# Decaying attention in front of two expert layers: leaving out the scores above the diagonal blocks, and letting the planner choose among ten plans

## The chip, the cores and the metric

One core of one Trainium2 chip runs the kernel, in one launch. The metric is the device time of that launch in microseconds (us). The engines are TensorE (PE: matmuls; its weight loads have a row of their own, PEld), VectorE (DVE), ScalarE (ACT), GpSimd (POOL) and SyncE (SP), which here only issues DMAs.

## What is computed

Three stages, one behind the other. The first is attention with a decay: for 2 batches and 8 heads of 64 columns, in blocks of 64 positions out of 768,

```python
intra = (qb @ kb.T * Dmask) @ vb          # Dmask = lam ** (i - j) for i >= j, else 0
inter = (qb * lam_pow) @ kv_state
out[block] = intra + inter
kv_state = lam ** 64 * kv_state + (kb * rev_pow).T @ vb
```

Then `x = out` as 1536 tokens of 512 columns goes through `(sigmoid(x @ w_gate) * (x @ w_val)) @ w_out` with 1536 hidden columns, and through `elu(x @ w_in) @ w_out2` with 2048.

## The kernel before

**Attention** goes in six chunks of 128 positions (`CH`; the loop of line 595), so two of the reference's blocks are one chunk, and the mask of a chunk is 128 by 128. Chunk `c` has two loads of 1 MB (`load`, line 535): `tin`, k and q with head columns on partitions, and `nat`, k and v with positions on partitions. For a chunk the program does:

- `scores` (line 582): for each batch, 16 fp32 matmuls give k by q of all heads, `st`, in two row tiles (heads in partitions 0 to 63 and 64 to 127) that write two PSUM banks, `A1` and `B1`. DVE multiplies each bank by the decay mask `da` into `pr`. The second batch uses the same two banks.
- `kd`, k with its decay, 8 ACT instructions; `ql`, q with its decay, 2 on POOL.
- `u`, 32 matmuls of `kd` by v into bank `C1`, and on DVE the state `sn` for the next chunk.
- `x`, 32 matmuls of v by `pr`, whole 128 by 128 blocks, into banks `xu_0` and `xu_1`, and from the second chunk on 32 more of the state by `ql` on top, these in four 64x64 tiles of the array (`x<-ql,sn` in the rows; `xs` below).
- `split_chunk` (line 444) reads `x` on ACT, DVE and POOL and makes the operands of the first expert layer, each split into a high and a low part (`x11h`, `x11l` and so on).

**The expert layers** multiply in fp32r, three matmuls for one product of split operands. `product` (line 479) is a seven-multiplication scheme for 2x2 blocks: groups M2, M5, M1, M4, M3, M7, M6 of six matmuls each. M2, M4, M7 add up in bank A, M5, M3, M6 in bank B, and M1 has bank C; between groups ACT and DVE read the banks. In the profile bank `A0` is called `warm`, since that tile came first. After chunks 1, 3 and 5 the products G and V (gate and value) of 256 columns of the first weight group run. `unit` (line 687) is the product with `w_out`: six matmuls of up to 512 columns into `xu`, two banks, which attention's `x` uses before. A weight block of 1 MB comes in as 64-bit words through one buffer `w64`, and `fetch` and `prep_sums` turn it into operands on ACT, DVE and POOL.

**Order.** Every operation is recorded by a helper, so all rows say line 177. `issue` (line 314) then makes the order of each engine's instructions: `run` (line 256) is a list scheduler with costs for each operation, used forward and backward five times in turn; the plan with the earliest end is kept. `together` makes one operation of a block of matmuls; `hazards` (line 200) finds who must wait for whom, for PSUM by bank and partition half. 24 matmuls on zeros (`warm<-idle`) are recorded ahead of all.

The buffers tie the stages together: `tin` and `nat` of chunk 3 go where those of chunk 0 were, chunk 4's where chunk 1's were, chunk 5's where chunk 3's were. `pr`, `ql` and `xa` lie in the buffers that the operands of `w_out` (`woh`, `wol`) take later.

Of the kernel before, what the change touches and what calls it, by code (L numbers as in the profile page):

```python
# [110 lines left out]
class Op:  # L111
    __slots__ = ("eng", "call", "reads", "writes", "gap", "took", "port", "table", "preds", "shape")
# [12 lines left out]
class Work:  # L125
# [10 lines left out]
    def cost(self, op, fn, args, kw):  # L136
# [4 lines left out]
        if op.eng == "tensor":  # L141
            dt = kw["rhs"].dtype
            op.shape = dt if dt != F32 else (kw["lhsT"].halves, kw["lhsT"].ix.size) if len(kw["rhs"].halves) < 2 else kw["lhsT"].ix.size
# [5 lines left out]
        if op.eng == "sync":  # L149
            return 440, n * P * 4 / 423  # L150
# [11 lines left out]
    def record(self, eng, fn, args, kw):  # L162
# [13 lines left out]
        def call():  # L176
            return getattr(getattr(self.nc, eng), fn)(*(real(a) for a in args), **{k: real(a) for k, a in kw.items()})  # L177
# [7 lines left out]
    def together(self, ways=2):  # L185
# [11 lines left out]
        op.call = lambda: [c() for c in calls][-1]  # L197
        self.ops.append(op)

    def hazards(self):  # L200
        write, read, banks, tables = {}, {}, {}, {1: [], 2: []}
        holder, users, freed = {}, {}, {}
        for k, op in enumerate(list(self.ops)):
# [46 lines left out]
            if op.table:  # L250
                before.update(tables[3 - op.table])
                tables[op.table].append(k)
            before -= {-1, k}
            op.preds = sorted(before)

    def run(self, preds, key, backward=False):
# [7 lines left out]
        at, start, end = [0.0] * n, [0.0] * n, [0.0] * n  # L264
        free = dict.fromkeys(ENGINES, 0.0)
        port = behind = queue = 0.0
        shape = table = None
        for k in range(n):
            if not left[k]:
                heapq.heappush(soon[ops[k].eng], (0.0, k))  # L270
        for _ in range(sum(op.eng is not None for op in ops)):
# [5 lines left out]
            k = heapq.heappop(ripe[e])[1]  # L277
            op = ops[k]
            if e == "sync":
                late = 300 if queue < t + 2000 else 1100  # L280
# [33 lines left out]
    def issue(self, tc, rounds=5):  # L314
# [7 lines left out]
        key, best = list(range(n)), None  # L322
        for _ in range(rounds):
            start, end = self.run(preds, key)
            if best is None or max(end) < best[0]:
                best = (max(end), start)
            _, back = self.run(turned, [-end[n - 1 - k] for k in range(n)], True)
            key = [-back[n - 1 - k] for k in range(n)]
        order = sorted(range(n), key=lambda k: (best[1][k], k))
        behind = mybir.DependencyInfo(mybir.DependencyClass.Sync, mybir.DependencyReason.DATA)  # L330
        port = None
        with tc.manual_schedule():
            for k in order:
                op = self.ops[k]
                made = op.call()
                if op.eng and op.port:
                    if op.eng == "vector":
                        port = made
                    elif port:
                        tc.add_manual_dep(made.ins, port.ins.name, behind, reason="shared port")  # L340
                        port = None
# [3 lines left out]
def tile_decay_attention_two_mlps(  # L345
# [133 lines left out]
    def product(kind, w, ops, sig, r, which, gsplit=None):  # L479
        s, t0, n = r  # L480
        bank, wt = {}, None
        for m in ORDER:
            x = BANK[m]
            if x not in bank:
                bank[x] = ps.tile([P, 512], F32, BANKS[which][x])[:, :n]
# [3 lines left out]
            first = m in ("M2", "M5", "M1")  # L489
# [4 lines left out]
            if m == "M2":  # L494
                wt = sb.tile([P, NS[which]], F32, f"wt{which}", bufs=2)[:, :n]
                nc.scalar.copy(wt, p)
            elif m == "M5":
# [27 lines left out]
    da = low[:, 0:1024].rearrange("p (q g n) -> p q g n", q=2, g=NP)  # L525
    lp = low[:, 1024:1536].rearrange("p (g n) -> p g n", g=NP)
    rev = da[:, :, :, CH - 1:CH]
    l_ch = lp[:, :, CH - 1:CH]

    lam_s = sb.tile([P, H + NP], F32, "lam")  # L530
    nc.sync.dma_start(out=lam_s, in_=lam2)
# [3 lines left out]
    def load(c):  # L535
        if c == 2:
            tin[c] = sb.tile([P, 2, 2, NP, CH], F32, "xPh1", name="tin2")
            nat_of[c] = sb.tile([P, 2, 2, H, D], F32, "sig1", name="nat2")
        else:
            tin[c] = sb.tile([P, 2, 2, NP, CH], F32, ("gh1", "gl1")[int(c in (1, 4))], name="tin")  # L540
        to = tin[c].rearrange("p b q g s -> p b (q g s)")
        for b in (slice(0, 1), slice(1, 2)) if not c else (slice(0, 2),):
            nc.sync.dma_start(out=to[:, b], in_=att[c, 0][:, b])
        nc.sync.dma_start(out=nat_of[c].rearrange("p b q h e -> p b (q h e)"), in_=att[c, 1])
# [11 lines left out]
    one = low[:, 1536:1536 + CH]  # L556
    nc.gpsimd.memset(one, 1.0)
    nc.gpsimd.affine_select(out=one, in_=one, pattern=[[1, CH]], compare_op=ALU.is_equal, fill=0.0,
                            base=1 - CH, channel_multiplier=1)
    for h in range(H):  # L560
        nc.vector.tensor_tensor_scan(out=da[:, h // NP, h % NP], data0=lam_s[:, h:h + 1].to_broadcast([P, CH]),
                                     data1=one, initial=0.0, op0=ALU.mult, op1=ALU.add)
    nc.vector.tensor_copy(lp[:, :, 0], lam_s[:, H:H + NP])
# [7 lines left out]
    for _ in range(24):  # L571
        nc.tensor.matmul(warm, lhsT=idle[:, :P], rhs=idle, start=True, stop=True)

    xops = [new_xops(0), new_xops(1)]
    kds, prs, sns, xas = {}, {}, {}, {}
# [3 lines left out]
    def half(q, p):  # L579
        return (q + p // 2) % 2  # L580

    def scores(c):
        prs[c] = []
        for b in range(2):
# [6 lines left out]
            for q in range(2):  # L591
                nc.vector.tensor_tensor(out=pr[:, q], in0=sts[q], in1=da[:, q], op=ALU.mult)
            prs[c].append(pr)

    for c in range(NCH):
        more = c + 1 < NCH
        s, t0 = (0, c * CH) if c < 2 else (1, (c - 2) * CH)
        scores(c)
        if more:
            kd = sb.tile([P, 2, H, D], F32, ("gh0", "gl0")[c % 2], name="kd")  # L600
            for h in range(H):
                nc.scalar.mul(kd[:, :, h], nat_of[c][:, :, 0, h], rev[:, half(h % 2, h // 2), h // 2])
        if c:
            ql = sb.tile([P, 2, NP, CH], F32, "wol_0", name="ql")
            for b in range(2):
                nc.gpsimd.tensor_tensor(out=ql[:, b], in0=tin[c][:, b, 1], in1=lp, op=ALU.mult)
        if more:
            u = ps.tile([P, 2, NP, D], F32, "C1", name="u")
            with nc.together():
                for b in range(2):  # L610
                    for p in range(NP):
                        for q in range(2):
                            nc.tensor.matmul(u[(lo, hi)[half(q, p)], b, p], lhsT=kd[:, b, 2 * p + q],
                                             rhs=nat_of[c][:, b, 1, 2 * p + q], start=True, stop=True)
            sn = sns[c + 1] = sb.tile([P, 2, NP, D], F32, f"wt1_{c % 2}", name="sn")
            if c == 0:
                nc.vector.tensor_copy(sn, u)
            else:
                for p in range(NP):
                    nc.vector.scalar_tensor_tensor(out=sn[:, :, p], in0=sns[c][:, :, p], scalar=l_ch[:, p],  # L620
                                                   in1=u[:, :, p], op0=ALU.mult, op1=ALU.add)
# [235 lines left out]
```

## Time and profile before

| | |
|---|---|
| time, median of 3 runs | 593.93 us (593.72 to 594.12) |
| the profiled execution's own time | 593.81 us |
| its span, first to last instruction | 592.1 us |
| what lies around the span | 1.7 us |
| PE, DVE, POOL, ACT busy | 98%, 66%, 53%, 51% of the span |
| DMA | 51.98 MB, 51.39 MB of it through one queue |

The ends of matmuls are modelled, so a busy PE is not PE at its peak: how long a block of matmuls takes is read from where it starts to where the next one starts. In the chain of work, a piece is such a stretch. A timeline row gives start and duration in us, then engine, operation, tiles (out<-in), shapes and count, and in brackets the idle time before it with what ended it.

### The profile page before, as it was taken

How to read it: one execution, taken by the hardware profiler on the slowest of the kernel's cores; microseconds unless marked ns; L12 is line 12 of the kernel's file. 1: busy time of each engine (PE TensorE's matmuls, PEld its weight loads, DVE VectorE, ACT ScalarE, POOL GpSimd, SP SyncE). 2: the span in 40 equal slices, each digit the busy share in tenths (PEclk: the TensorE clock that was granted, in tenths of full speed). 3: DMA queues.
4: the chain of work that ended last, by engine and by line, in shares of the span. 5: the costliest groups of instructions: out<-in, count | busy, mean ns of one | idle time of the engine just before them, and what ended most of it. 6: DMA issues, size and time to landing. Idle time of an engine off the chain costs nothing.

```text
span 592.1 us, 9322 instructions
## 1 busy us (share of the span) xinstructions
PE 582.0 (98%) x3632; PEld 496.2 (84%) x3632; DVE 389.6 (66%) x690; ACT 300.5 (51%) x571; POOL 313.3 (53%) x264
## 2 busy tenths in 40 slices
PE   9999989999999999999999999999999999999997
PEld 5788878888888888888898888887888888888886
DVE  5978653566467457457548985667666777777484
ACT  3884356543343244243247988755636454646160
POOL 2778398478476376367237884563805446361100
PEclk9999999999999999999999999999999999999999
DMA  8945022222212211122202202312221111110004
GB/s 320 417 190 214 2 71 73 81 103 102 72 71 72 71 72 72 71 73 71 72 2 72 72 0 83 132 72 71 72 72 43 53 53 68 72 71 1 0 37 178
DMA packets 8828, 51.98 MB, mean 88 GB/s; under 512 B 1104, under 2 KB 1360, under 8 KB 3024
## 3 DMA queue, kind: packets, MB, share of 16 engines
q1 hardware_dynamic: 8784, 51.39, 23.5%
q8 instruction: 28, 0.46, 0.3%
q14 instruction: 16, 0.13, 0.1%
HBM read 48.24 MB, written 3.15 MB: 87 GB/s over the span
## 4 chain that ended last, share of the span: by engine, by line
PE 85%; ACT 4%; DMA 4%; DVE 4%; POOL 3%; issue 1%; ACTq 0%; POOLq 0%; SPq 0%; DVEq 0%
PE xu L177 37%; PE B L177 19%; PE A L177 11%; PE warm L177 10%; PE C L177 6%; DMA w<-in_w_val 2%; DMA w<-in_w_in 2%; ACT w L177 1%; PE x L177 1%; DVE sums L177 1%; PE st L177 1%; ACT sig L177 1%; POOL l L177 1%; DVE w L177 1%; ACT kd L177 1%
## 5 line engine op out<-in xcount | busy, mean ns | idle before, releaser
L177 PE MATMUL xu<-gh,woh 128*128 128x512 f32 (+1 forms) x322 | 126.0, 395 | 1.6 <-DVE xt L177 1.4
L177 PE MATMUL xu<-gl,woh 128*128 128x512 f32 (+1 forms) x322 | 126.0, 391 | 0.0
L177 PE MATMUL xu<-gh,wol 128*128 128x512 f32 (+1 forms) x322 | 125.3, 389 | 0.0
L177 DVE TENSOR_TENSOR acc<-xu,acc 128x512 f32<-128x512 f32 x120 | 81.2, 687 | 39.9 <-PE xu L177 39.0
L177 POOL TENSOR_TENSOR gl<-sig,gh 128x1024 fp32r<-128x1024 f32 (+1 forms) x38 | 73.2, 1938 | 53.3 <-ACT gh L177 33.3
L177 POOL TENSOR_TENSOR t<-w 128x512 f32<-128x512 f32 (+1 forms) x80 | 69.0, 889 | 42.7 <-DVE w L177 40.0
L177 POOL TENSOR_TENSOR l<-t,h 128x768 fp32r<-128x768 f32 (+1 forms) x38 | 61.0, 1615 | 41.3 <-DVE w L177 19.7
L177 PEld LDWEIGHTS xu<-gh,woh 128*128 128x128 f32 x322 | 60.5, 188 | 15.6 <-DVE xt L177 1.4
L177 PEld LDWEIGHTS xu<-gh,wol 128*128 128x128 f32 x322 | 60.5, 188 | 12.1
L177 PEld LDWEIGHTS xu<-gl,woh 128*128 128x128 f32 x322 | 60.6, 188 | 11.8 <-POOL gl L177 1.2
L177 POOL TENSOR_TENSOR wol<-w,woh 128x512 fp32r<-128x512 f32 x26 | 33.1, 1293 | 59.8 <-ACT woh L177 59.2
L177 ACT CAST gh<-sig 128x512 fp32r<-128x512 f32 (+1 forms) x58 | 45.2, 784 | 33.9 <-DVE sig L177 32.5
L177 ACT ACTIVATE w<-w 128x1024 f32<-128x1024 f32 x34 | 38.6, 1135 | 34.8 <-POOL wol L177 18.2
L177 DVE SCALAR_TENSOR_TENSOR w<-w,w 128x1024 uint32<-128x1024 uint32 x34 | 46.5, 1367 | 0.3
L177 DVE TENSOR_TENSOR wt<-B,wt 128x256 f32<-128x256 f32 (+1 forms) x45 | 22.9, 509 | 33.7 <-PE B L177 31.7
L177 DVE TENSOR_SCALAR w<-w 128x1024 uint32<-128x1024 uint32 x34 | 31.2, 916 | 21.0 <-ACT w L177 20.6
L177 ACT ACTIVATE sig<-B 128x256 f32<-128x256 f32 (+1 forms) x62 | 28.3, 456 | 29.5 <-PE B L177 24.2
L177 ACT ACTIVATE sig<-warm 128x256 f32<-128x256 f32 x36 | 13.9, 385 | 49.1 <-DVE warm L177 24.5
L177 DVE TENSOR_TENSOR wt<-C,wt 128x256 f32<-128x256 f32 (+1 forms) x45 | 23.0, 511 | 18.9 <-PE C L177 18.3
L177 ACT ACTIVATE sig<-sig 128x256 f32<-128x256 f32 (+1 forms) x68 | 34.5, 507 | 1.6
L177 ACT CAST h<-t 128x512 fp32r<-128x512 f32 (+1 forms) x40 | 29.1, 728 | 8.7 <-PE B L177 4.5
L177 POOL TENSOR_TENSOR l<-w,h 128x256 fp32r<-128x256 f32 x36 | 26.7, 752 | 9.5 <-ACT h L177 4.1
(143 smaller groups left out, 1477.1 us busy)
## 6 DMA issues: line engine op xcount, KB each, us to landing
w<-in_w_out SPq DMA_DIRECT2D x14, 1024.0 KB, 4.8
w<-in_w_in SPq DMA_DIRECT2D x8, 1024.0 KB, 4.7
nat<-in_att SPq DMA_DIRECT2D x6, 1024.0 KB, 11.7
w<-in_w_gate SPq DMA_DIRECT2D x6, 1024.0 KB, 5.3
w<-in_w_val SPq DMA_DIRECT2D x6, 1024.0 KB, 4.9
tin<-in_att SPq DMA_DIRECT2D x5, 1024.0 KB, 12.1
out_t<-o SPq DMA_DIRECT2D x11, 256.0 KB, 2.0
tin<-in_att SPq DMA_DIRECT2D x2, 512.0 KB, 5.0
```

The costliest lines, as they stand in the source:

```text
L177: return getattr(getattr(self.nc, eng), fn)(*(real(a) for a in args), **{k: real(a) for k, a in kw.items()})
```

## The change

- **Scores in 64-position blocks.** Of a chunk's 128 by 128 scores of a head, the three 64 by 64 blocks that the mask doesn't zero are made, with 64x64 tiles of the array, four at a time. The work is grouped by four heads (`g`) of both batches in place of one batch: group 0 uses banks `A1`, `B1`, group 1 `C0`, `C1`. A group is 16 matmuls, eight of 128 columns and eight of 64. `pr` has 3/4 of the elements.
- **`x`** is made in two parts: the first 64 positions from one 64 by 64 block (16 matmuls of 64 rows, four tiles), the others from all 128 rows (16 matmuls with 64 columns out).
- **`u` of chunk c-1** is made in `scores(c)`, in two halves, in columns 384 to 511 of the score banks. For chunk 1 ACT copies it (four instructions) where DVE had one.
- A small ACT instruction per chunk stands between the first part of `x` and the matmuls of the state (`fence`).
- **`product`, in the attention stage,** goes M5, M2, M1, ... on two banks: M1 has the second half of bank B (`two=True`).
- **`unit`** of the first weight group puts its first eight results into banks `C0`, `C1`.
- **Loads** of chunks 0 to 2 come in halves of 512 KB; `lam` is loaded through ACT's queue. Loads of chunks 3, 4, 5 are recorded behind `scores` of chunks 1, 2, 4 (before: behind chunks 0, 1, 3).
- The mask is set up by eight scans (four of 128, four of 64 columns), six ACT copies.
- 18 matmuls on zeros in place of 24.
- **The planner** tries ten settings of two new parameters (`stick`: stay with a matmul shape; `ahead`: don't start an operation long before it is due), seven rounds each, takes the DMA queue as busy until 3.5 us, and counts each change between matmul forms as before (150 ns).

```diff
-    def issue(self, tc, rounds=5):
+    def issue(self, tc, rounds=7):
...
+        best = None
+        for stick in (0, 1500, 4000, 10000, 20000):
+            for ahead in (8e3, 20e3):
+                key, gate, least = list(range(n)), None, 1e9
+                for _ in range(rounds):
+                    start, end = self.run(preds, key, gate=gate, stick=stick)
...
-    def product(kind, w, ops, sig, r, which, gsplit=None):
+    def product(kind, w, ops, sig, r, which, gsplit=None, two=False):
...
-        for m in ORDER:
+        for m in ("M5", "M2") + ORDER[2:] if two else ORDER:
...
+                if two and x == 2:
+                    bank[x] = bank[1, "rest"]
...
+            for cols in (slice(0, 1024), slice(1024, 2048)) if c < 3 else (slice(0, 2048),):
+                nc.sync.dma_start(out=to[:, cols], in_=src[:, cols])
...
-            pr = sb.tile([P, 2, NP, CH], F32, f"woh_{b}", name="pr")
-            sts = [ps.tile([P, NP, CH], F32, bank, name="st") for bank in ("A1", "B1")]
-            with nc.together():
-                for p in range(NP):
-                    for st, r in zip(sts, (lo, hi)):
-                        nc.tensor.matmul(st[:, p], lhsT=tin[c][r, b, 0, p], rhs=tin[c][r, b, 1, p], start=True, stop=True)
...
+        for g in range(2):
+            pr = sb.tile([P, 2, 2, 3, 64], F32, f"woh_{g}", name="pr")
+            banks = [ps.tile([P, 512], F32, bank, name="st") for bank in (("A1", "B1"), ("C0", "C1"))[g]]
+            sts = [t[:, 0:384].rearrange("p (b t n) -> p b t n", b=2, t=3) for t in banks]
+            with nc.together(4):
+                for b in range(2):
+                    k, q = (tin[c][:, g, b, i].rearrange("p i (t n) -> p i t n", n=64) for i in range(2))
+                    for full in (True, False):
+                        for st, r in zip(sts, (lo, hi)):
+                            for p in range(2):
+                                at = (hi, lo) if full == (p == 0) else (lo, hi)
+                                ts = (slice(0, 3, 1 + p) if p else slice(0, 2)) if full else slice(1 + p, 2 + p)
+                                nc.tensor.matmul(st[at[0], b, ts], lhsT=k[r, p, int(full)],
+                                                 rhs=q[r, p] if full else q[r, p, 1:2], start=True, stop=True)
+            u = [t[:, 384:512].rearrange("p (b e) -> p b e", b=2) for t in banks]
+            if c:
+                with nc.together():
...
+                                nc.tensor.matmul(u[i][(lo, hi)[half(q, i)], b], lhsT=kds[c - 1][:, b, h],
+                                                 rhs=nat_of[c - 1][:, 1, b, h], start=True, stop=True)
...
+                            nc.tensor.matmul(xs[i][r, b, g, 0:64], lhsT=nat_of[c][at, 1, b, 2 * p + q],
+                                             rhs=prs[c][g][at, half(q, p), b, 0], start=b == 0 and g == 0 or not c,
...
+                            nc.tensor.matmul(xs[i][r, b, g, 64:128], lhsT=nat_of[c][:, 1, b, 2 * p + q],
+                                             rhs=prs[c][g][:, half(q, p), b, 1 + i], start=not c,
...
+            nc.scalar.mul(low[:, 1667 + c:1668 + c], low[:, 1664:1665], 1.0)
+            work.ops[-1].fence = quads
...
-            product("G", wG, xops, sig, r, 0)
-            product("V", wV, xops, sig, r, 0)
+            product("G", wG, xops, sig, r, 0, two=True)
+            product("V", wV, xops, sig, r, 0, two=True)
...
-        units(wo, g, adder(acc, i == 1))
+        units(wo, g, adder(acc, i == 1), early=2 if i == 1 else 0)
```

## Rows read from the trace of the kernel before

**Rows 1.** The page's busy time: engine, us, share of the span, instructions.
```profile
PE 582.0 (98%) x3632; PEld 496.2 (84%) x3632; DVE 389.6 (66%) x690; ACT 300.5 (51%) x571; POOL 313.3 (53%) x264
```

**Rows 2.** Stretches of the span: length, busy us of PE, PEld, DVE, ACT, POOL, clock, DMA.
```profile
7.10:25.70 18.60, 17.68 (x250) 13.54 (x249) 13.85 (x26) 12.95 (x38) 9.34 (x8) 1.00 1.01 423
25.70:39.10 13.40, 12.69 (x174) 10.90 (x170) 10.49 (x24) 11.06 (x28) 9.56 (x8) 1.00 0.70 283
39.10:72.80 33.70, 33.20 (x430) 29.71 (x430) 25.89 (x65) 14.37 (x34) 21.57 (x16) 1.00 0.31 114
...
98.00:310.00 212.00, 212.00 (x1163) 184.27 (x1162) 123.06 (x195) 85.31 (x143) 120.97 (x106) 1.00 0.21 75
310.00:350.00 40.00, 38.75 (x235) 33.92 (x235) 36.20 (x86) 33.98 (x79) 32.41 (x31) 1.00 0.16 53
...
440.00:588.70 148.70, 148.62 (x734) 124.98 (x732) 102.64 (x159) 71.51 (x121) 50.50 (x38) 1.00 0.15 54
```

**Rows 3.** The chain that ended last, in order of time: start, us, what.
```profile
21.58 11.48 DMA w<-in_w_val
...
39.64 1.08 PE u L177 x32
...
43.39 1.09 PE st L177 x16
46.47 2.93 PE x L177 x64
...
60.12 1.02 PE x L177 x16
...
66.11 1.03 PE x L177 x32
```

**Rows 4.** Timeline, 3 to 26 us: ahead of the first product G.
```profile
3.20 0.71 SPq L177 DMA_DIRECT2D w<-in_w_gate  x1
...
18.03 3.77 ACT L177 ACTIVATE kd<-nat,low 128x128 f32<-128x128 f32 x12
...
18.48 2.79 PE L177 MATMUL u<-nat,kd 128*64 128x64 f32 x31
...
23.19 0.60 ACT L177 CAST h<-t 128x512 fp32r<-128x512 f32 x1
...
25.75 0.38 PE L177 MATMUL warm<-x11h,h 128*128 128x256 f32 x1
```

**Rows 5.** Timeline, 34 to 40 us: ahead of the first product V.
```profile
34.32 1.28 ACT L177 ACT_TABLE_LOAD   x1
...
38.66 0.42 ACT L177 ACTIVATE sig<-warm 128x256 f32<-128x256 f32 x1
...
39.13 0.39 PE L177 MATMUL warm<-x11h,h 128*128 128x256 f32 x1 [0.30 <-ACT sig L177]
```

**Rows 6.** Timeline, 50 to 53 us: from the first product V to the second G.
```profile
50.15 0.28 PE L177 MATMUL B<-xPh,l 128*128 128x256 f32 x1
...
50.47 0.43 DVE L177 TENSOR_TENSOR B<-B,wt 128x256 f32<-128x256 f32 x1 [0.28 <-PE B L177]
...
52.13 0.42 DVE L177 TENSOR_TENSOR sig<-B,sig 128x256 f32<-128x256 f32 x1
```

**Rows 7.** Timeline of PE, 72 to 77 us: the end of attention.
```profile
72.83 1.10 PE L177 MATMUL x<-ql,sn 64*64 64x128 f32 x32
74.72 0.39 PE L177 MATMUL warm<-x11h,h 128*128 128x256 f32 x1 [0.79 <-ACT x11h L177]
...
76.61 0.47 PE L177 MATMUL xu<-gh,woh 128*128 128x512 f32 x1 [0.45 <-DVE xt L177]
```

**Rows 8.** The tile `pr`: ns min/median/max, first and last start.
```profile
L177 DVE TENSOR_TENSOR pr<-st,low x24: 676/682/693, 8.3 to 70.0; 128x512 f32<-128x512 f32 x24
```

**Rows 9.** The tile `x`, the same columns.
```profile
L177 DVE TENSOR_TENSOR x22l<-x,x22h x6: 416/417/419, 17.1 to 76.4; 128x256 fp32r<-128x256 f32 x6
```

**Rows 10.** The page's DMA issues: count, KB of each, median us to landing.
```profile
w<-in_w_out SPq DMA_DIRECT2D x14, 1024.0 KB, 4.8
```

More of the change, by code (lines that the diff above doesn't have):

```diff
@@ L111, with __init__ @@
 class Op:
-    __slots__ = ("eng", "call", "reads", "writes", "gap", "took", "port", "table", "preds", "shape")
+    __slots__ = ("eng", "call", "reads", "writes", "gap", "took", "port", "table", "preds", "shape", "fence")
+    def __init__(self):
+        self.fence = None
 class Engine:
@@ L184, in together @@
     @contextmanager
-    def together(self, ways=2):
+    def together(self, ways=2, fence=None):
         self.block = []
@@ L252, in hazards, with run @@
                 tables[op.table].append(k)
+            if op.fence:
+                before.add(self.ops.index(op.fence))
             before -= {-1, k}
             op.preds = sorted(before)
-    def run(self, preds, key, backward=False):
+    def run(self, preds, key, backward=False, gate=None, stick=0):
         ops = self.ops[::-1] if backward else self.ops
@@ L263, in run @@
         ripe, soon = {e: [] for e in ENGINES}, {e: [] for e in ENGINES}
-        at, start, end = [0.0] * n, [0.0] * n, [0.0] * n
+        at, start, end = [max(0.0, g) for g in gate] if gate else [0.0] * n, [0.0] * n, [0.0] * n
         free = dict.fromkeys(ENGINES, 0.0)
-        port = behind = queue = 0.0
+        port = behind = 0.0
+        queue = 3500.0
         shape = table = None
@@ L321, in issue @@
                 turned[n - 1 - x].append(n - 1 - k)
[L322 to L328, printed above, removed]
+        best = None
[4 more added lines that the diff above has]
+                    start, end = self.run(preds, key, gate=gate, stick=stick)
+                    least = min(least, max(end))
+                    if best is None or max(end) < best[0]:
+                        best = (max(end), start)
+                    _, back = self.run(turned, [-end[n - 1 - k] for k in range(n)], True)
+                    key = [-back[n - 1 - k] for k in range(n)]
+                    gate = ahead and [least + k - ahead for k in key]
         order = sorted(range(n), key=lambda k: (best[1][k], k))
         behind = mybir.DependencyInfo(mybir.DependencyClass.Sync, mybir.DependencyReason.DATA)
-        port = None
+        port, made = None, {}
         with tc.manual_schedule():
@@ L334, in issue @@
                 op = self.ops[k]
-                made = op.call()
+                made[op] = op.call()
+                for m in made[op.fence][-4:] if op.fence else ():
+                    tc.add_manual_dep(made[op][0].ins, m.ins.name, behind, reason="row tiles of a bank")
                 if op.eng and op.port:
                     if op.eng == "vector":
-                        port = made
+                        port = made[op][0]
                     elif port:
-                        tc.add_manual_dep(made.ins, port.ins.name, behind, reason="shared port")
+                        tc.add_manual_dep(made[op][0].ins, port.ins.name, behind, reason="shared port")
                         port = None
@@ L488, in product @@
             bh, bl = (v[:, :, t0:t0 + n] for v in x_operand(ops, s, m))
-            first = m in ("M2", "M5", "M1")
+            first = m in ("M2", "M5") or m == "M1" and not two
             for k in range(2):
@@ L605, in tile_decay_attention_two_mlps @@
[L605 to L608, printed above, removed]
+            ql = sb.tile([P, 2, 2, 2 * CH], F32, "wol_0", name="ql")
+            for g in range(2):
+                nc.gpsimd.tensor_tensor(out=ql[:, g], in0=tin[c][:, g, :, 1].rearrange("p b i n -> p b (i n)"),
+                                        in1=lp2[:, g:g + 1].to_broadcast([P, 2, 2 * CH]), op=ALU.mult)
@@ L609, in tile_decay_attention_two_mlps @@
+        for g in range(2):
             with nc.together():
                 for b in range(2):
[L611 to L621, printed above, removed]
@@ L748, in tile_decay_attention_two_mlps, with units @@
     BY_T = [(c, t) for t in range(3) for c in range(KC)]
-    def units(wo, g, done, order=BY_T):
+    def units(wo, g, done, order=BY_T, early=0):
         for c, t in order:
-            unit(wo, g, c, t, done)
+            unit(wo, g, c, t, done, tags=("C0", "C1") if t < early else None)
     g = new_g()
```

179 lines of the change are left out of this document (112 added, 67 removed).

## The prediction

> **What bounds the kernel.** I read the page's busy time first, then the stretches, then the chain for the length of each block of matmuls, and the timeline where a stretch shows PE waiting. PE is busy 98% of the span, no other engine over 66% [rows 1]. From 98 us on nothing waits that matters: PE is busy 212.00 of 212.00 us and 148.62 of 148.70, and lacks 1.25 us in the 40 us from 310 [rows 2]. The change touches only the order there. So the reader looks at the first 98 us, where attention and the first products G and V lie, and sees three parts. Up to 25.75 us, where the first product G starts, data and weight preparation set the pace: the DMA engines are full (share 1.01, 423 GB/s) [rows 2], and PE spends 2.79 us on a block of `u` that takes 1.08 elsewhere, because `kd` comes one at a time from ACT [rows 3, 4]. From there to 39.13 us, the first V, the weights of V are late: their load takes 11.48 us [rows 3], and ACT, busy 11.06 of 13.40 us [rows 2], has a 1.28 us table load ahead of the activation that frees bank A [rows 5]. From 39.13 us PE is all but full (33.20 of 33.70) [rows 2], up to the end of attention, where two matmuls' waits, 0.79 and 0.45 us, end on ACT and DVE [rows 7]. The granted clock is 1.00, the upper of its two levels (2.4 GHz), in every stretch [rows 2]. A microsecond of PE work removed behind 39.13 us is therefore worth nearly a microsecond; one removed ahead of it only if later work can be drawn into the hole, or V starts earlier.
>
> **What a block of matmuls costs.** `x` with 32 matmuls takes 2.93 - 1.03 = 1.90 us (a piece of 64, less its 32 of the state), with 16 it takes 1.02 [rows 3]: 55 ns a matmul, and 0.14 us for each block (the change of form). Taking 0.14 off the others: `st` 59 ns, 119 for a pair of tiles with 128 columns; `u` 29 ns, 59 for a pair with 64 columns; the 64x64 tiles of the state 28 ns, 111 for a set of four with 128 columns [rows 3]. So a set of matmuls side by side costs 110 to 119 ns with 128 columns and 59 with 64, whether there are two or four of them. No row shows four tiles with 64 columns: if columns decide, a set costs 59 ns; if there is a cost of each matmul, it can't be seen below 28 ns, and a set costs 112.
>
> **Scores.** Before, two blocks, 2.18 us a chunk. After, two blocks with four sets of 128 columns and four of 64: 4 x 0.111 + 4 x 0.059 + 0.28 = 0.96 us; at 28 ns each, 32 x 0.028 + 0.28 = 1.18. Saved 1.00 to 1.22.
>
> **x.** Before 1.90. After, four sets of four with 64 columns (0.24) and eight pairs with 64 (0.47), or 0.90 at 28 ns each, in two to four blocks (0.28 to 0.56): 0.99 to 1.46. Saved 0.44 to 0.91.
>
> **u** is the same work in two blocks instead of one: 0.14 more. The state's matmuls stay. A chunk thus saves 1.3 to 2.0 us of PE. I take 1.6, near the middle, as the sets of 128 columns, which have a row, carry most of it.
>
> The Trainium skill speaks against this edit (TensorE: Matmul & The Clock Gate, "Wait — 56ns, not 53.3ns?"): start to start never drops below about 25 ns, and with hardware decoding off each matmul costs about 62 ns of the sequencer. By the 62 ns the 64 matmuls of scores and `x` would take 4.0 us a chunk, as much as before, and nothing would be saved. Rows 3 decide against that: 32 matmuls of the state in 1.03 us are at most 32 ns each.
>
> **Other engines.** `pr` falls from 512 to 384 elements. By 682 ns for 512 and 417 for 256 [rows 8, 9] an element is 1.04 ns, so 24 instructions save 0.13 us each, 3.2 us of DVE. ACT gets four copies of state (0.31 us each, by 3.77 for 12 `kd` [rows 4]), five small instructions as fences (at most as long, 1.6 us) and six set-up copies. The set-up lies ahead of the first `pr` at 8.3 us [rows 8], under the first load; without that cover it costs 6 x 0.31 = 1.9 us at the start. The fence waits on PE, and `xa` and `kd` queue behind it on ACT; PE then waits for it ahead of the state's matmuls. That hand-over is hidden by the second part of `x`, 0.47 us or more; else it costs about the 0.30 us of such a wait [rows 5] five times. It is in the bounds below.
>
> **Loads.** The halves are five more DMA issues on SP, 0.71 us each at most [rows 4], 3.6 us together. The 7.3 MB of chunks 0 to 2 and the gate weights need 17 us at 423 GB/s [rows 2], so bytes, not issues, set the landing: nothing. If that cover is gone, chunk 2 comes up to 3.6 us late.
>
> **The sum**, against the profiled execution's 593.81 us, 0.12 below the median of the runs.
> (a) Chunks 3, 4, 5 lie behind 39.13 us, as all but half of chunk 3's scores do: 3 x 1.6 = 4.8 (3.9 to 6.0).
> (b) Chunks 0 to 2 free 4.8 us ahead of it, and `u` of chunk 1, now part of `scores(2)`, no longer stands ahead of `x` of chunk 1 and holds PE for 2.79 - 1.08 = 1.7. Chunk 3 can be drawn into that hole: it costs 0.96 + 1.22 + 1.22 + 1.03 = 4.4 us after the change. None to all of it moves, as ACT is 83% busy there. I take 3.0.
> (c) V may start earlier. Its weights' load could at best take 4.8 us, as others do [rows 10], not 11.48: 0 to 6.7. But the queue in front of it is the same bytes. I take 1.0.
> (d) At the end of attention PE waits 0.79 and 0.45 us [rows 7], 1.2 together; `unit` in `C0`, `C1` needs no `xu`, but still needs `wol`, which POOL makes behind `ql`. 0 to 1.2, I take 1.0.
> (e) Products on two banks. M5 is now first in bank B, which M6 leaves last: the last M6 matmul is at 50.15, its add at 50.47, the multiply that empties the bank ends at 52.55 [rows 6], 2.1 us that something else must fill. Five boundaries: 0 to 10.5 us lost. Attention blocks and `unit` fill most; I take 1.5 lost.
> (f) The new plan elsewhere: it can win at most the 1.3 us that PE lacks [rows 2], and lose as much. 0.5 won.
> 4.8 + 3.0 + 1.0 + 1.0 - 1.5 + 0.5 = 8.8. **593.8 - 8.8 = 585.0 us.**
>
> **Rivals.**
> *V's weights come early* (0.20). With another DMA model the plan may issue V's weights ahead of a chunk's load, and V starts 4 us earlier, well within the 6.7; then (c) gives 3.0 more, (d) 0.2 and, with every boundary filled, (e) 1.5: 8.8 + 4.7 = 13.5, so 580.3. For it: the 11.48 us are a queue. Against: V's start also hangs on ACT [rows 5].
> *The other engines take the place* (0.15). PE's freed time turns into waits: DMA at share 1.01, ACT 83%, then DVE 25.89 of 33.70 [rows 2]. Then (b), (c), (d), (f) are nothing, half of (a) stays, and (e) falls into the same waits: 593.8 - 2.4 = 591.4. Against: behind 39.1 us ACT is busy only 14.37 of 33.70.
> *The two-bank products stall PE* (0.12), the other side. Bank B now takes M5, M1, M3 and M6, with one group of six matmuls on bank A between them, and the reading instruction alone is 0.42 us [rows 6]. While DVE is 77% busy, it comes late. Five boundaries at the full 2.1 us plus six products with three inner waits of 0.1 are 12.3; less the 1.5 counted, 10.8: 593.8 - 8.8 + 10.8 = 595.8. It decides from 8.8 us above the 1.5 on, that is 1.7 us unfilled at each boundary beside the inner waits. The Trainium skill (PSUM — Partial Sum Buffer, "PSUM bank collisions raise a hardware error") asks for guards by bank, not by address, and the planner does so: M1's half waits as if it were M5's. No run here shows the hardware's part of it.
>
> **Chances.** The forecast has 0.53, with its own range 581 to 589. Range over all: 578 to 593, which leaves out the two-bank rival and most of the far end of the early V. About 0.2% (1.2 us) is what a measurement of this kernel tells from no change. Faster by more: nearly all of the forecast (0.52), early V (0.20), two thirds of the other engines' (0.10): 0.82. Slower: the two-bank rival, 0.11. Same: 0.07.
>
> **What would show it.** A block of 16 `st` at 0.48 to 0.59 us between starts; `x` under 1.5 us a chunk; first G at 23 to 24 us (the operand that it waits for, `h<-t`, is cast at 23.19 [rows 4]); first V at 38 with most of chunk 3 in front of it; `xu` within 1.5 us of the last state block. Wrong if `st` stays near 1 us a block, if PE waits over 0.5 us in front of a B group at each product, if the granted clock falls below 1.00 where the shorter filler ends ahead of the data, or if PE's idle time from 98 us on grows by more than 2 us.

## The result and the profile after

The changed kernel takes 587.70 us (median, 587.27 to 588.17), the kernel before took 594.02 beside it (593.72 to 595.06): ratio 0.9891, 95% interval 0.9873 to 0.9908. It is 6.3 us faster; 8.8 were forecast. The profiled execution took 588.17 us.

The page of the changed kernel, its head and busy time, answers to [rows 1]:

```profile
span 586.4 us, 10067 instructions
...
PE 572.8 (98%) x4010; PEld 492.1 (84%) x4010; DVE 383.9 (65%) x689; ACT 300.3 (51%) x586; POOL 311.7 (53%) x265
...
PEclk9989999999999999999999999999999999999999
```

The span is 5.7 us shorter, but PE's busy time fell by 9.2. So PE is idle longer than before: 13.6 us instead of 10.1. (Six filler matmuls `warm<-idle` fewer count in both.) The clock row shows a dip that was not there before. Stretches of the changed kernel, columns as in [rows 2]:

```profile
11.00:36.00 25.00, 19.50 (x529) 16.54 (x530) 17.41 (x37) 19.04 (x53) 16.42 (x13) 0.93 0.94 378
12.40:15.80 3.40, 2.90 (x49) 1.99 (x43) 1.86 (x6) 3.40 (x13) 3.40 (x4) 0.51 1.04 407
36.30:39.70 3.40, 3.40 (x42) 3.18 (x44) 1.35 (x3) 0.38 (x1) 0.00 (x0) 0.51 0.02 5
...
310.00:350.00 40.00, 39.50 (x247) 35.29 (x246) 38.02 (x90) 33.51 (x79) 30.35 (x26) 1.00 0.11 31
```

The lost time lies between 11 and 36 us: PE is busy 19.50 of 25.00. In 310 to 350 it is busier than before (39.50 against 38.75). The granted clock is at its lower level, 1.2 GHz, from 12.4 to 15.8 and from 36.3 to 39.7 us; before it was 1.00 in every stretch [rows 2]. That is one execution of each: over all timed executions the mean clock was 0.993 to 1.000 in the kernel before and 0.993 to 0.996 in the changed one, so the clock dips in some executions of the kernel before too. Waits of PE from 7 to 98 us in the changed kernel: in total, times, longest:

```profile
PE x L180 <- DVE low L180: 2.6, 1, 2.6
PE x L180 <- issue: 2.2, 1, 2.2
PE st L180 <- issue: 2.2, 1, 2.2
PE st L180 <- DMA tin<-in_att: 0.5, 1, 0.5
PE B L180 <- DVE x22l L180: 0.4, 1, 0.4
PE B L180 <- ACT sig L180: 0.2, 1, 0.2
```

Two waits of 2.2 us have "issue" beside them: no engine and no load of data is named as what held PE. The timeline of PE in the changed kernel shows where they are, with the price of the new blocks of matmuls:

```profile
10.98 1.94 PE L180 MATMUL x<-pr,nat 64*64 64x64 f32 x64 [2.61 <-DVE low L180]
...
20.71 0.65 PE L180 MATMUL x<-ql,sn 64*64 64x128 f32 x11
23.57 0.77 PE L180 MATMUL x<-ql,sn 64*64 64x128 f32 x19 [2.20 <-issue]
...
26.12 0.38 PE L180 MATMUL warm<-x11h,h 128*128 128x256 f32 x1
...
32.70 0.64 PE L180 MATMUL st<-nat,kd 128*64 128x64 f32 x14
35.51 0.27 PE L180 MATMUL st<-nat,kd 128*64 128x64 f32 x2 [2.17 <-issue]
...
36.90 0.41 PE L180 MATMUL warm<-x143l,h 128*128 128x256 f32 x1
37.11 0.41 PE L180 MATMUL warm<-x143h,l 128*128 128x256 f32 x1
...
43.99 0.69 PE L180 MATMUL x<-pr,nat 64*64 64x64 f32 x32
44.50 0.85 PE L180 MATMUL st<-tin 64*64 64x128 f32 x32
45.28 0.39 PE L180 MATMUL warm<-x11h,h 128*128 128x256 f32 x1
...
45.95 1.15 PE L180 MATMUL x<-pr,nat 128*64 128x64 f32 x32
46.93 0.64 PE L180 MATMUL st<-nat,kd 128*64 128x64 f32 x16
47.50 0.39 PE L180 MATMUL warm<-x11h,l 128*128 128x256 f32 x1
47.72 0.28 PE L180 MATMUL warm<-x11h,h 128*128 128x256 f32 x1
47.84 0.28 PE L180 MATMUL warm<-x11l,h 128*128 128x256 f32 x1
...
56.58 1.78 PE L180 MATMUL x<-pr,nat 64*64 64x64 f32 x64
58.28 0.39 PE L180 MATMUL B<-x22h,h 128*128 128x256 f32 x1
...
72.22 1.10 PE L180 MATMUL x<-ql,sn 64*64 64x128 f32 x32
73.25 0.50 PE L180 MATMUL st<-gh,woh 128*128 128x512 f32 x1
```

Both halts fall in the middle of a block: 11 and 14 of its matmuls have begun, and the rest, with nothing new to wait for, begin 2.2 us later. From start to start the first part of `x`, 32 matmuls, takes 0.51 us, a group of scores with 32 takes 0.78, the second part of `x` 0.98, half of `u` 0.57. In a later chunk both parts of `x` in one row take 1.70 (56.58 to 58.28). The 256-column matmuls at 36.90 and 37.11, in the second dip of the clock, start 0.21 us apart, those at 47.72 and 47.84 0.12. The first product G starts at 26.12, V at 45.28. At the end of attention the first `unit` follows 1.03 us behind the start of the last state block.

### The profile page after: what moved, and what is told of

It reads as the page before. It is cut to its first block, busy times and chain, and to the rows that moved or that the text cites. A ratio compares the mean times of both kernels' runs of the same rounds, so it can differ in the third digit from the quotient of the medians.

```text
span 586.4 us, 10067 instructions
## 1 busy us (share of the span) xinstructions
PE 572.8 (98%) x4010; PEld 492.1 (84%) x4010; DVE 383.9 (65%) x689; ACT 300.3 (51%) x586; POOL 311.7 (53%) x265
## 4 chain that ended last, share of the span: by engine, by line
PE 87%; DVE 4%; ACT 3%; DMA 3%; issue 2%; POOL 1%; SPq 0%; DVEq 0%; ACTq 0%
PE xu L180 34%; PE st L180 30%; PE B L180 10%; PE warm L180 10%; PE x L180 3%; DMA tin<-in_att 2%; DVE w L180 1%; ACT sig L180 1%; DMA w<-in_w_in 1%; DVE sums L180 1%; ACT w L180 1%; DVE wt L180 0%; POOL gl L180 0%; DVE sig L180 0%; SPq L180 0%
## 5 line engine op out<-in xcount | busy, mean ns | idle before, releaser
L180 POOL TENSOR_TENSOR t<-w 128x256 f32<-128x256 f32 (+1 forms) x80 | 69.6, 895 | 103.6 <-DVE w L180 64.3
L180 PE MATMUL xu<-gh,woh 128*128 128x512 f32 (+1 forms) x306 | 119.1, 394 | 0.3
L180 PE MATMUL xu<-gl,woh 128*128 128x512 f32 (+1 forms) x306 | 119.2, 390 | 0.0
L180 PE MATMUL xu<-gh,wol 128*128 128x512 f32 (+1 forms) x306 | 118.9, 388 | 0.0
L180 PEld LDWEIGHTS xu<-gh,woh 128*128 128x128 f32 x306 | 57.4, 188 | 13.1 <-DVE acc L180 0.7
L180 PE MATMUL st<-x143l,h 128*128 128x512 f32 (+1 forms) x150 | 51.7, 346 | 0.0
L180 PE MATMUL st<-x143h,l 128*128 128x512 f32 (+1 forms) x150 | 51.3, 346 | 0.0
L180 PE MATMUL st<-x143h,h 128*128 128x512 f32 (+1 forms) x150 | 51.2, 347 | 0.0
L180 ACT ACTIVATE sig<-st 128x512 f32<-128x512 f32 (+1 forms) x52 | 29.3, 565 | 36.4 <-PE st L180 20.8
L180 DVE TENSOR_TENSOR wt<-st,wt 128x512 f32<-128x512 f32 (+1 forms) x57 | 31.9, 560 | 20.2 <-PE st L180 19.8
## 6 DMA issues: line engine op xcount, KB each, us to landing
tin<-in_att SPq DMA_DIRECT2D x3, 1024.0 KB, 12.4
```

What stands on the lines that cost most here:

```text
L180: return [getattr(getattr(self.nc, eng), fn)(*(real(a) for a in args), **{k: real(a) for k, a in kw.items()})]
```

## The experiments

### Whose gain is it: the plan's or attention's?

The theory was that attention's fewer columns carry the gain; the rival, that the planner does, which now tries ten settings and keeps the best.

**The new planner alone**: the kernel before, with the classes Op, Engine and Work of the changed one.

```diff
-        key, best = list(range(n)), None
-        for _ in range(rounds):
+        best = None
+        for stick in (0, 1500, 4000, 10000, 20000):
+            for ahead in (8e3, 20e3):
...
-        port = behind = queue = 0.0
+        port = behind = 0.0
+        queue = 3500.0
```

> Attention as before, with the new planner alone (its costs, its ten settings, seven rounds). Theory 1 (PE's accounts: of the 5.6 us between the first and the last matmul 4.0 are columns that attention no longer streams, 3.8 are PE time lost behind 98 us that the new plan lost less of, and 2.2 were lost more ahead of it): the planner alone gives 3 to 4 us, 590 to 591 us. Rival A (the plan is all, and the smaller blocks give nothing): 588 us. Rival B (the plan gives nothing; the smaller loss behind 98 us follows from attention ending otherwise): 593 to 595 us.

590.02 us, 0.9934 (0.9922 to 0.9946): 4.0 us faster than before with attention untouched. Its page's busy time:

```profile
PE 579.4 (98%) x3632; PEld 496.2 (84%) x3632; DVE 386.3 (66%) x690; ACT 298.6 (51%) x571; POOL 314.3 (53%) x264
```

The same 3632 matmuls are 2.6 us less busy than in [rows 1], and at a span of 588.7 PE is idle 9.3 us instead of 10.1. In 310 to 350 us, the place from which the prediction took its limit of 1.3 us, PE's busy time is the same (38.70 us against 38.75). The stretch from 98 us to the end, columns as in [rows 2], of the kernel before, of the planner alone and of the changed kernel:

```profile
98.00:600.00 502.00, 489.10 (x2593) 419.21 (x2591) 320.74 (x536) 246.36 (x446) 250.58 (x212) 1.00 0.19 68
98.00:600.00 502.00, 486.09 (x2586) 417.44 (x2584) 318.38 (x535) 243.22 (x444) 251.18 (x212) 1.00 0.19 68
98.00:600.00 502.00, 484.40 (x2585) 417.03 (x2583) 320.58 (x538) 243.46 (x446) 251.35 (x212) 1.00 0.19 68
```

Behind 98 us all three do the same kind of work, matmuls of 256 and 512 columns. Those that begin there are 995 and 1596 before, 991 and 1593 with the planner alone, 996 and 1587 in the changed kernel. Most of them start 0.120 and 0.227 us apart in all three traces. At that spacing they need 481.7, 480.5 and 479.8 us (an estimate from these counts); the last one begins 490.6, 487.2 and 484.9 us behind 98 us. So PE lost 8.9, 6.7 and 5.1 us there, though it is marked busy nearly throughout. Up to its last matmul the profiled execution with the planner alone is 3.4 us ahead of the kernel before, 2.3 of them won behind 98 us and 1.2 ahead of it. The changed kernel is 5.7 us ahead, 3.8 and 1.9.

**Attention alone**: the changed kernel with the old planner's settings (how it tells matmul forms apart stays the new way).

```diff
-        for stick in (0, 1500, 4000, 10000, 20000):
-            for ahead in (8e3, 20e3):
+        for stick in (0,):
+            for ahead in (0,):
...
-        queue = 3500.0
+        queue = 0.0
...
-                late = 300 if queue < t + 2000 or t < 3000 else 1100
+                late = 300 if queue < t + 2000 else 1100
...
-    def issue(self, tc, rounds=7):
+    def issue(self, tc, rounds=5):
```

> The changed attention, products and units with the planner as it was (one setting, five rounds, its first estimate of the loads). Theory 1: 4.0 us of columns are gained and some of it lost again in the first 40 us, nothing is gained behind 98 us: 590 to 592 us. Rival A (the plan is all): 594 us. Rival B (the plan gives nothing): 587 to 588.5 us.

592.85 us, 0.9984 (0.9969 to 0.9999; 591.40 to 596.99 over 12 runs): 1.2 us faster, barely told from nothing, and between the range of the theory and that of rival A. On top of the new planner attention's edit is worth 590.02 - 587.70 = 2.3. So of 6.3 us the planner gives 4.0 and attention 2.3, and the rival was nearer. Taken in the other order attention gives 1.2 and the planner 5.2 (592.85 to 587.70), so the split hangs on the order.

### What holds PE at "issue"?

Windows that begin at 0 count the matmuls (PE) and weight loads (PEld) begun. Those of the changed kernel end within its two halts (22.50 and 34.00) and at five other moments:

```profile
0.00:11.20 11.20, 7.40 (x92) 3.44 (x96) 6.37 (x24) 4.19 (x8) 0.89 (x7) 1.00 0.79 294
0.00:17.40 17.40, 13.11 (x225) 7.78 (x226) 10.40 (x33) 9.34 (x24) 5.32 (x11) 0.90 0.88 334
0.00:22.50 22.50, 17.07 (x349) 11.24 (x350) 13.78 (x38) 13.59 (x38) 8.67 (x14) 0.92 0.91 352
0.00:23.60 23.60, 17.10 (x353) 11.27 (x354) 13.78 (x38) 13.59 (x38) 8.67 (x14) 0.93 0.91 355
0.00:29.90 29.90, 22.78 (x480) 16.21 (x482) 18.45 (x51) 17.83 (x49) 13.73 (x18) 0.94 0.94 369
0.00:34.00 34.00, 26.21 (x604) 19.37 (x605) 21.57 (x60) 21.92 (x60) 16.36 (x20) 0.95 0.94 370
0.00:36.10 36.10, 26.80 (x609) 19.89 (x610) 23.61 (x60) 23.23 (x61) 17.31 (x20) 0.95 0.89 351
```

PE halts with 699 and with 1209 instructions begun, 510 apart. Between 22.50 and 23.60 DVE, ACT and POOL add nothing to their busy time either (13.78, 13.59, 8.67): none of them is at work that PE could be waiting for. At the other five moments PE has begun 188, 451, 707, 962 and 1219: some 256 in each 6.2 us. The page's queues show what comes in such portions:

```profile
q8 instruction: 31, 0.51, 0.4%
```

That is 31 packets of 16.5 KB, one for 8020 / 31 = 259 of PE's instructions (the kernel before has 28 for 7264, also 259). The trace holds these packets with their times. In the changed kernel they start at 14.71, 21.13, 27.16 and 33.14 us, 6.0 to 6.4 us apart, and each moves for 0.95 to 1.13 us. The second and the fourth fall into the two halts: they land at 22.21 and 34.27, and PE goes on 1.4 and 1.2 us later, at 23.57 and 35.51. The queue's line in the DMA view of 21 to 22.5 us, and below it of 33 to 34.4 us:

```profile
q8 instruction: 1, 0.02, 4.5%
q8 instruction: 1, 0.02, 5.0%
```

The theory: PE's own instructions come in portions of 256, and while the loads fill the DMA engines (share 0.94) one comes every 6.2 us. Before, PE needed 9.5 us for 256 there (499 instructions in 18.60 us [rows 2]) and never ran out. The rival: the halts belong to what the plan put there.

**48 more instructions ahead**: the changed kernel in its very order, with 24 tiny matmuls ahead of the first filler (two instructions each).

```diff
+                for _ in range(24):
+                    work.nc.tensor.matmul(warm[:, 0:16].ap(), lhsT=idle[:, 0:P].ap(), rhs=idle[:, 0:16].ap(), start=True, stop=True)
+                return filler()
```

> The changed kernel with its very order, and 24 matmuls of 16 columns on zeros ahead of the first filler (48 more PE instructions, weight loads counted, done before the data come). In the changed kernel PE stands still 2.5 us inside a block of the state's matmuls and 2.4 us inside a block of u, where no engine works, with 705 and 1217 matmuls and weight loads begun, which are 193 + 512 and 193 + 1024. Theory 1 (PE waits for its own instructions, which come in packets of 16 KB, 256 of them): the halts stay at 705 and 1217 begun, so 48 instructions earlier in the program, inside blocks of x or st; the time stays within 1 us of 587.7. Rival (a wait for another engine's work, or the hand-over of the fence): the halts stay in the same two blocks, with 753 and 1265 begun.

587.15 us, 0.9876 (0.9856 to 0.9897). The padded kernel's PE timeline, and below it the window that ends within its first halt:

```profile
19.35 1.31 PE L180 MATMUL x<-pr,nat 64*64 64x64 f32 x36
23.12 0.57 PE L180 MATMUL x<-pr,nat 128*64 128x64 f32 x12 [2.46 <-issue]
...
35.77 0.51 PE L180 MATMUL x<-pr,nat 128*64 128x64 f32 x10 [2.09 <-issue]
```

```profile
0.00:22.50 22.50, 16.28 (x348) 11.76 (x350) 13.18 (x38) 13.64 (x38) 8.65 (x14) 0.92 0.89 353
```

The halts moved to other matmuls, into the blocks of `x<-pr`, and came at the same counts, 698 and 1207. A third stop, of 1.5 us put down to "issue", came at 952, between the two. The count decides, not the work. The time is that of the changed kernel.

**Light loads**: the changed kernel in its order; the loads of chunks 3 and 4 move 128 of 2048 columns.

```diff
+                if c in (3, 4):
+                    work.ops[-1].call = lambda to=to, src=src: [work.nc.sync.dma_start(out=to[:, 0:128].ap(), in_=src[:, 0:128])]
```

> The changed kernel with its very order; of the loads of chunks 3 and 4 only 128 of 2048 columns are moved (the rest of the output's attention for those chunks is computed on what lay in the buffers). Theory 1 (instruction packets stand behind the loads in the DMA engines): from 24 us on, where the engines are no longer full, a packet of 256 instructions is on its way 0.5 to 1 us after it is asked for in place of 3.5, the halt at 1217 begun goes, that at 705 may stay, and the time falls by 1.5 to 4 us, to 584 to 586. Rival (the halts are the plan's, and the data of chunks 3 and 4 come early enough anyway): both halts stay, 587 to 588.5 us.

584.41 us, 0.9839 (0.9824 to 0.9854), 3.3 us below the changed kernel. Stretches of the light kernel:

```profile
11.00:24.00 13.00, 10.11 (x290) 8.72 (x293) 7.67 (x15) 9.39 (x30) 7.78 (x7) 0.87 1.02 402
24.00:36.00 12.00, 11.56 (x314) 10.66 (x310) 10.13 (x24) 10.18 (x26) 8.80 (x7) 1.00 0.08 24
```

The first halt, still under full DMA engines, stayed (2.27 us); the second is gone. With the DMA engines at 0.08, 624 instructions took 12.00 us, 4.9 for 256. Behind the first halt, which ends at 23.45, the next packet starts 1.1 us later, at 24.55; in the changed kernel it started 3.6 us behind the halt's end (23.57 to 27.16). The clock's second dip is gone too, but so it is in the padded kernel, where the second halt stayed. Halt and dip could account for the 3.3 us between them: the halt is 2.17, and a stretch of 3.40 us at half the clock costs up to 1.7 (0.21 against 0.12 us from start to start). No run parts the two.

**A planner that counts instructions**, ten settings: 256 of PE's instructions not sooner than 6.2 us after the last 256, 5.0 from 30 us on.

```diff
+        told, edge, entered = 0, 193, 0.0
...
+                told += op.count
+                if told > edge and not backward:
+                    t = max(t, entered + (6200 if entered < 30000 else 5000))
+                    entered, edge = t, edge + 256
```

> The changed kernel, where the planner also counts PE's instructions and lets each 256 of them begin no earlier than 6.2 us behind the 256 before (5.0 us from 30 us on), as the changed kernel's trace shows them. Theory 1 (the plan doesn't know of this wait, puts other engines' work behind it, and loses more than the wait itself): 1 to 3 us faster than the changed kernel, 584.5 to 586.7. Rival (the wait can't be planned around, as nothing else is ready): 587 to 588.5 us.

588.97 us, 0.9911 (0.9894 to 0.9927). A miss: in the profiled execution the clock stayed at 1.000, but PE still waits 5.7 us at "issue" in front of blocks of `st` and `x`, and the plan that was best of the ten by the planner's reckoning is no better on the chip than the changed kernel's.

**The same with 54 settings** and 14 rounds. Without the count, this wider search ends at the changed kernel's own order.

```diff
-        for stick in (0, 1500, 4000, 10000, 20000):
-            for ahead in (8e3, 20e3):
+        for stick in (0, 700, 1500, 3000, 5000, 7500, 10000, 14000, 20000):
+            for ahead in (0, 5e3, 8e3, 12e3, 20e3, 40e3):
```

> The planner that counts PE's instructions, with 54 settings and 14 rounds in place of ten and seven; without that count the wider search ends at the very plan of the changed kernel. Theory 1 (instruction packets set PE's pace up to 36 us, and a plan that knows it can place slow matmuls there): 585 to 587 us, faster than the changed kernel. Rival (as the narrow search, 588.97: nothing else is ready): 587.5 to 589.5 us.

**584.47 us**, 0.9836 (0.9822 to 0.9849): faster than both kernels, 3.2 us under the changed one. Two of its stretches, and below them its PE timeline at the halt:

```profile
11.00:36.00 25.00, 22.66 (x526) 18.26 (x526) 18.46 (x43) 20.16 (x54) 17.26 (x14) 1.00 0.94 377
36.00:98.00 62.00, 62.00 (x840) 55.89 (x839) 39.99 (x91) 34.34 (x79) 45.06 (x34) 1.00 0.27 95
```

```profile
20.95 0.73 PE L182 MATMUL st<-tin 64*64 64x128 f32 x20
23.34 0.55 PE L182 MATMUL st<-tin 64*64 64x128 f32 x12 [1.65 <-issue]
```

That is below the range of the theory. One halt is left, 1.65 us, again with 700 instructions begun, and in the profiled execution the clock never falls. (Two of the other four have a mean clock of 0.996 and are no slower, 584.36 and 584.41, so the dip alone does not make the difference.) From 11 to 36 us PE begins as many instructions as in the changed kernel (1052 against 1059), and the packets start within 0.4 us of the same times: the portions set that number. But from 36 to 98 us PE is busy without a gap, at the upper clock.

**That planner with the attention of before**, to see whether attention's edit gains from it.

```diff
+        told, edge, entered = 0, 193, 0.0
...
+        for stick in (0, 700, 1500, 3000, 5000, 7500, 10000, 14000, 20000):
+            for ahead in (0, 5e3, 8e3, 12e3, 20e3, 40e3):
```

> Attention as before, with the planner of the last kernel (PE's instructions counted, 54 settings, 14 rounds). Theory 1 (the smaller blocks are worth their 4.0 us of columns only where the plan knows of the instruction packets, which 256 slow instructions a chunk hardly meet): 588 to 590 us, so 4 to 5 us behind the same planner with the changed attention (584.47), against 2.3 us with the changed kernel's planner. Rival (the wide search is what gained, and attention's change gives as little as before): 585.5 to 587.5 us.

586.82 us, 0.9888 (0.9871 to 0.9904). The rival's range held. The wider planner gives the old attention 3.2 us as well (590.02 to 586.82), though at 9.5 us for 256 instructions the count hardly binds there: without the count the planner arrives at the very same order. So for the old attention the 3.2 us come from the wider search; for the new one the search without the count would have found nothing. Attention's edit is worth 2.3 again (586.82 to 584.47; 3.1 by the ratios 0.9888 and 0.9836, each to the kernel before beside it).

### Do the banks cost what was feared?

**Three banks for a product**: M1 has a bank of its own, `C0`, which the second group of scores uses too.

```diff
-            product("G", wG, xops, sig, r, 0, two=True)
-            product("V", wV, xops, sig, r, 0, two=True)
+            product("G", wG, xops, sig, r, 0)
+            product("V", wV, xops, sig, r, 0)
```

> The changed kernel, with M1 of the attention stage's products in a bank of its own again (C0, which the scores of group 1 use too) and M2 first. Theory 1 (two banks cost PE little, other work fills the boundaries): 586.5 to 590 us, and the blocks between two products keep their waits. Rival (two banks stall PE by 1.5 us or more in all, as term (e) of the prediction had it): faster than 586.2 us.

601.01 us, 1.0107 (1.0088 to 1.0125): slower than either range. **One set of score banks**: both groups on `A1`, `B1`, three banks for the products, `unit` without `early`.

```diff
-            banks = [ps.tile([P, 512], F32, bank, name="st") for bank in (("A1", "B1"), ("C0", "C1"))[g]]
+            banks = [ps.tile([P, 512], F32, bank, name="st") for bank in ("A1", "B1")]
```

> The changed kernel with both score groups on banks A1 and B1, M1 in bank C0 and M2 first as before, units in xu alone. Theory 1 (the second set lets scores go on while DVE reads the first, and the price of two-bank products is small): a group of scores waits for the two multiplies of the one before, about 1.0 us of DVE, six times and more: 589 to 592 us. Rival (the sets give nothing, the two-bank products cost 1.5 us): 586 to 587.5 us.

595.21 us, 1.0025 (1.0013 to 1.0036): slower than either range again. Waits of PE from 7 to 98 us in the kernel with one set:

```profile
PE st L180 <- DVE pr L180: 3.6, 1, 3.6
PE st L180 <- ACT sn L180: 1.7, 2, 1.4
```

The scores wait 5.3 us for the banks, until DVE's `pr` and ACT's `sn` have read them. In the changed kernel that wait isn't in the list, and the two-bank products wait 0.2 us for a bank, behind ACT's `sig`. (The 0.4 us in front of `B` is for the operand `x22l`; before, with three banks, the same wait was 0.3.) Giving the third bank to the scores is worth 7.5 us as planned here (595.21 to 587.70). Both kernels also change the plan, so the figures are not the banks' alone, and what made the three-bank kernel so slow was not settled.

**Without `early`**: the first units use the banks of before.

```diff
-        units(wo, g, adder(acc, i == 1), early=2 if i == 1 else 0)
+        units(wo, g, adder(acc, i == 1), early=0)
```

> The changed kernel, with all units in the xu banks, so that none can start ahead of the reading of x. Theory 1 (the two extra banks closed the hole at the end of attention, where PE went on at once behind the last state block): PE stands 1 to 2 us behind the last state block again, 588.7 to 589.7 us. Rival (the plan finds other work for the hole): 587.2 to 588.2 us.

588.03 us, 0.9897 (0.9883 to 0.9911), the time of the changed kernel within its interval. As the rival had it, the plan found other work for the end of attention: behind the last state block, which starts at 68.44 us, products run up to the first `unit` at 74.04, and that waits 0.4 us.

### Do the halves matter?

```diff
-            for cols in (slice(0, 1024), slice(1024, 2048)) if c < 3 else (slice(0, 2048),):
+            for cols in (slice(0, 2048),):
```

**Whole loads in the changed kernel:**

> The changed kernel with the loads of chunks 0 to 2 in one piece of 1 MB each. Theory 1 (bytes, not the pieces, set when a chunk can start, and PE's instruction packets set the pace from 11 to 36 us anyway): 587 to 588.5 us, the first x block within 1 us of 10.98. Rival (halves let chunk 0 start earlier, and that reaches the end): 589 us or more.

586.23 us, 0.9866 (0.9852 to 0.9879), faster than either range. **Whole loads with the planner of 54 settings:**

> The last planner and the changed attention, with the loads of chunks 0 to 2 in one piece. Theory 1 (pieces don't matter; the 586.2 of whole loads was another plan's luck): 583.5 to 586 us. Rival (whole loads give the 1.5 us again): 582 to 583.4 us.

587.81 us, 0.9897 (0.9883 to 0.9912), slower than either range, although PE waits only 1.1 us at "issue". (Its profiled execution has the clock at the lower level from 10.7 to 17.5 and from 24.4 to 27.8 us.) Whole loads are 1.5 us better under one planner and 3.3 worse under the other: no effect of their own is shown. Each edit draws another plan, and plans of the same work lie up to 4.5 us apart (584.47 and 588.97).

## Why the prediction came out where it did

The direction and the range held, and 587.70 lies near the 585.0. But that is in part luck: terms were off in opposite ways. Of the 8.3 us of (a) to (e) attention's edit gave 2.3, 6.0 too few, and the plan gave 3.5 more than (f) had.

**Term (f), the new plan elsewhere: 0.5 us forecast, "at most 1.3", 4.0 measured** with the planner alone (2.3 of it behind 98 us, in the profiled execution). This is the step that failed most. It read the limit from PE's idle time behind 98 us. But "busy" holds lost time as well: with the same 3632 matmuls the planner took 2.6 us out of PE's busy time and 0.8 out of its idle time. By the spacing of its matmuls PE lost 8.9 us behind 98 us before, not 1.3; the planner alone won 2.3 of them, the changed plan 3.8. Changes of form can't be the reason, as behind 98 us all matmuls have one form (128*128). The largest part of the difference lies between matmuls of 256 columns that follow one another: beyond 0.120 us each they took 4.1 us in all before, 2.7 with the planner alone, 1.2 in the changed kernel. What they waited for there was not settled.

**Term (a), attention behind V: 4.8 us forecast, 2.3 to 2.9 by the lengths of the blocks** (3 x 0.76 to 0.97). The prediction counted the new sets by the program's calls and priced them by the trace's matmuls. One fp32 call is two matmuls in the trace: a group of scores has 32, not 16. (The section on the kernel before counts matmuls as the trace does, the one on the change counts calls.) Scores fell from 2.18 to 2 x 0.78 = 1.56 us a chunk, `x` from 1.90 to 0.51 + 0.98 = 1.49 or to 1.70, and `u` rose by 2 x 0.57 - 1.08 = 0.06: 0.76 to 0.97 saved instead of 1.6. With twice the sets the prediction's own prices give 8 x 0.111 + 8 x 0.059 + 0.28 = 1.64 for the scores, close to the 1.56. Columns decide, as it had chosen: 32 matmuls of 64 columns in 0.51 us are 16 ns each, below its bound of 28.

The Trainium skill (TensorE: Matmul & The Clock Gate, "Wait — 56ns, not 53.3ns?") has a floor of about 25 ns from start to start. The trace doesn't agree: these 32 matmuls, spread over four tiles, start 16 ns apart on average, and the slowest of the blocks above, half of `u`, takes 36 ns a matmul (0.57 us for 16), below the 62 ns of its other figure.

**Terms (b) to (e): 3.5 us forecast, nothing or a loss measured.** They were not measured one by one. Attention's 2.3 less (a) leave 0 to -0.6; the intervals of the two times are 0.7 and 1.0 us either way. And only 0.7 of the 2.3 were won ahead of 98 us, where (a) to (e) lie: there 479.8 us of work were left instead of 480.5 with the planner alone. Less (a), that is a loss of 1.6 to 2.2 us in the profiled executions. (b) asked PE to do more work ahead of 39 us, and the instructions for it didn't come in time: first G at 26.12 instead of 23 to 24, 4.4 us of halts in all. (c) V began at 45.28, not 38; the plan put attention first. (d) happened as described (a unit 1.03 us behind the last state block), but leaving it out costs 0.3 us, less than the noise, not 1.0. Of (e), 1.5 us, waits of 0.2 for a bank show.

**The rivals.** V didn't come early. The two-bank products don't stall. "The other engines take the place" was right that freed time turns into waits and wrong in whose: PE waited for itself. The prediction had named the sign that the clock might fall behind shorter filler. It fell at 12.4 us behind a wait of 2.61 us for `low`, and at 36.3 behind the second halt; behind the first halt of 2.20 us it did not.

What stays open: why a packet that moves in 1.1 us starts so late when the loads are in flight, what won the time behind 98 us, and how much of the 54-setting planner's 3.2 us the missing halt and dip carry, and how much its other choices.

## What to carry to other kernels

Count matmuls as the trace counts them, before pricing a set by the trace. A change that makes many small matmuls out of few also makes PE's instruction stream denser: where loads fill the DMA engines, work out how long 256 of its instructions last, and look for waits put down to "issue" in the middle of a block and for a packet of instructions in the DMA view there. PE's idle time is no limit to what another order can win: count the matmuls left at a mark, multiply by their usual spacing, and compare with the time they took. Run a new planner alone before crediting the work it orders: here it was worth more than the edit, and plans of one and the same work differed by up to 4.5 us (new attention) and 7.2 us (old, 594.02 to 586.82).

## What the runs showed of the hardware

PE got 256 instructions in 6.2 us while the DMA engines were at a share of 0.94, and halted 1.5 to 2.46 us when it needed them sooner; in the changed kernel the packets started 6.0 to 6.4 us apart, moved for 0.95 to 1.13 us, and PE went on 1.2 and 1.4 us behind the landing. With the engines at 0.08 it had 256 in 4.9 us without a halt in that stretch. A 64x64 tile of 64 columns costs 16 ns when four tiles take turns (0.51 us for 32, the change of form included). PE ran at 1.2 GHz from 12.4 to 15.8 and from 36.3 to 39.7 us, behind stops of 2.61 and 2.17 us, and with the planner alone from 74.8 to 78.3 us, behind waits of 1.25 and 0.45 us.
